# The last block of a routed expert layer: 32 tokens with weights stationary, in place of a half block of 128

## The chip, the cores and the metric

The kernel runs on one core of one Trainium2 chip. The metric is the device time of one execution in microseconds (us). TensorE (PE) multiplies matrices, VectorE (DVE) and ScalarE (ACT) work on elements, GpSimd (POOL) computes and issues indirect DMAs, SyncE (SP) issues the other DMAs. A matmul has a stationary operand, which a weight load (PEld, LDWEIGHTS) brings into the array, and a moving operand, whose columns stream through it.

## The reference

Attention with queries pooled in pairs of neighbouring dimensions, and behind it a mixture of eight experts of which each token takes one. The change is in the experts:

```python
def _moe_ref(x, modality_id, w_gate, modality_bias, w1, w2):
    logits = x @ w_gate + modality_bias[modality_id]
    e_idx = np.argmax(logits, axis=1)
    ...
    gate_w = probs[np.arange(N), e_idx]
    for e in range(E):
        mask = e_idx == e
        h = np.maximum(x[mask] @ w1[e], 0.0)
        out[mask] = gate_w[mask, None] * (h @ w2[e])
```

There are 4608 tokens of 512 floats, eight experts, and 1024 hidden values in each.

## The kernel before, in words

The first two thirds are the attention. From some 740 us on the kernel works on **blocks** of tokens that have one expert. The router on VectorE counts the tokens of each expert. An expert with n tokens gets full blocks of 256, and where a rest remains, either another full block or, for a rest of at most 128, a **half block** of 128 places. The program has a fixed list, `order`: full blocks 0 to 17 and then one half block, `NBF`, which is number 18 in this text. Whatever routing asks for beyond that list goes by a general path behind it, inside `tc.If(more > 0)`; `more` is column 2 of the tile `tot` (L425 to L430). Lists in DRAM name the tokens of each block; places beyond a block's tokens have an index out of range, and the scatter writes nothing for them.

Every product is made in three fp16 matmuls: activations and weights are each split into a high and a low part (`xh`/`xl`, `hi`/`lo`, `hh`/`hl`), and high·high, high·low and low·high are summed in PSUM. Weights arrive as f32 by DMA (`load_w`, from SP) in eight pieces to a block, four for each layer; `split_w` makes their two parts, `hi` on ScalarE (L1268) and `lo` on VectorE (L1269). Second-layer parts rotate through five buffers (`W2B`).

For a full block, `gemm1` makes a quarter of the hidden values with the weights stationary and 256 tokens moving (24 matmuls a quarter, L1285 to L1287); ScalarE writes `hh` by a relu (L1290), VectorE the rest `hl` (L1291). `gemm2` makes the second layer with the hidden values stationary and 512 output columns of the weights moving (L1331 to L1333): a call takes a quarter of the hidden values, and for each of two pieces of it both token halves in turn. `scaled` multiplies one half by the gate on ScalarE (L1339), and `scatter` writes its 128 rows to `out` by an indirect DMA that GpSimd issues (L1342).

`run_blocks` writes the order out by hand: eight steps `s` to a block, four of each layer. Beside them it issues the splits of weights that are needed a block later, DMAs, the gathers of tokens of the block after next (`load_x` at step 3, L1173, on GpSimd), and at step 5 (`T_ST`) the second scatter of the block before. Behind step 7 come both evictions of the block and its first scatter. Inside these blocks no engine is free to reorder; each runs its instructions as written. After block 17, `run_blocks` issues that block's second scatter, a DRAIN on GpSimd (`nc.gpsimd.drain(fusable=False)`, L1410), and the split of the last weight piece.

The half block is then made by `block(NBF)`. Its first layer is `half_gemm1` (L1293 to L1319) with tokens stationary and 256 columns of the weights moving: 48 matmuls, a relu into f32 (L1316), and eight f32 transposes on TensorE (L1304) with their split into `hh` and `hl` (L1306, L1307). Its second layer is `gemm2` for one half: 24 matmuls with 512 columns. One eviction and one scatter follow, and the program ends when that has landed.

Of the kernel before, what the change touches and what calls it, by code (L numbers as in the profile page):

```python
# [9 lines left out]
F32 = mybir.dt.float32  # L10
F32R = mybir.dt.float32r
F16 = mybir.dt.float16
BF16 = mybir.dt.bfloat16
I32 = mybir.dt.int32
# [84 lines left out]
NTT = T // P  # L99
TB = 256  # L100
HB = TB // 2
NBF = (T + E * (HB - 1)) // TB
NBST = 18
WR = 5
# [52 lines left out]
def drain(g):  # L157
    for _ in g:
        pass


class Router:
# [244 lines left out]
    def other_blocks(self):  # L407
        nc, sm = self.nc, self.sm
        rest = sm.tile([P, E], F32, name="rest")
        nc.vector.scalar_tensor_tensor(rest, self.na, -float(TB), self.base, op0=ALU.mult, op1=ALU.add)  # L410
        nc.vector.tensor_single_scalar(rest, rest, float(HB - 1), op=ALU.add)
        counts = sm.tile([P, 2, E], F32, name="nbh")
        nb, nh = counts[:, 0], counts[:, 1]
        self.up_to(rest, nb)
        yield
        nc.vector.scalar_tensor_tensor(nh, nb, -float(TB), rest, op0=ALU.mult, op1=ALU.add)
        nc.vector.tensor_single_scalar(nh, nh, float(HB - 1), op=ALU.is_gt)
        cum = self.running(counts, "cumB")
        cumB, cumH = cum[:, 0], cum[:, 1]
        yield  # L420
        self.ownB = self.owners(cumB, NBF - NA, "B")
        yield
        self.ownH = self.owners(cumH, E, "H")
        self.tot = self.con.tile([P, 3], I32, name="tot")
        nc.vector.tensor_single_scalar(self.tot[:, 0:1], cumB[:, E:E + 1], float(NA), op=ALU.add)  # L425
        nc.vector.tensor_copy(self.tot[:, 1:2], cumH[:, E:E + 1])
        most = sm.tile([P, 2], F32, name="most")
        nc.vector.tensor_scalar(most[:, 0:1], cumB[:, E:E + 1], float(NA), float(NBST), op0=ALU.add, op1=ALU.max)
        nc.vector.tensor_scalar(most[:, 1:2], cumH[:, E:E + 1], 1.0, -float(NBST + 1), op0=ALU.max, op1=ALU.add)
        nc.vector.tensor_tensor(self.tot[:, 2:3], most[:, 0:1], most[:, 1:2], op=ALU.add)  # L430

        yield
        done = sm.tile([P, E], F32, name="done")
        nc.vector.tensor_tensor(done, nb, self.na, op=ALU.add)
        full = sm.tile([P, E], F32, name="fulls")
        nc.vector.tensor_tensor(full, cumB[:, 0:E], self.na, op=ALU.subtract)
        half = sm.tile([P, E], F32, name="halfs")
        nc.vector.tensor_single_scalar(half, cumH[:, 0:E], float(2 * (NBF - NA)), op=ALU.add)
        nc.vector.tensor_single_scalar(half, half, 0.5, op=ALU.mult)
        nc.vector.tensor_tensor(half, half, done, op=ALU.subtract)  # L440
        nc.vector.tensor_tensor(half, half, full, op=ALU.subtract)
        self.done, self.full, self.half = done, full, half
# [756 lines left out]
def experts(tc, ctx, rt, ident, pre, w1, w2, out, side, first):  # L1199
# [93 lines left out]
    def half_gemm1(j):  # L1293
# [24 lines left out]
                turn_h(q - 1)  # L1318
        turn_h(3)  # L1319

    def gemm2(j, q, halves=(0, 1)):
        b = B[j]
        if q == 0 and halves[0] == 0:
            b["po"] = [ps_o.tile([P, DM], F32, name="po") for h in parts(j)]
        hi, lo = b["w", 4 + q]
        for f in range(2):
            c = 2 * q + f
            for h in halves:
                po = b["po"][h]
                hs = slice(h * P, (h + 1) * P)  # L1330
                nc.tensor.matmul(po, b["hh"][:, c, hs], hi[:, f], start=c == 0, stop=False)  # L1331
                nc.tensor.matmul(po, b["hh"][:, c, hs], lo[:, f], start=False, stop=False)
                nc.tensor.matmul(po, b["hl"][:, c, hs], hi[:, f], start=False, stop=c == 7)  # L1333
            beside()
# [3 lines left out]
        o = b["o", h] = xp.tile([P, DM], F32, name=f"o{h}")  # L1338
        nc.scalar.activation(o, b["po"][h], AF.Copy, scale=b["gate"][:, h:h + 1])  # L1339

    def scatter(j, h):
        nc.gpsimd.indirect_dma_start(out=out[:, :], out_offset=bass.IndirectOffsetOnAxis(ap=index(rt, j, h)[1], axis=0),  # L1342
                                     in_=B[j]["o", h][:, :], in_offset=None, bounds_check=T - 1, oob_is_err=False)

    def store(j, halves=(0, 1)):
        for h in halves:
# [13 lines left out]
    def run_blocks():  # L1360

        todo = iter(pieces[NF:])

        def fetch(n=1):
            for _ in range(n):
                p = next(todo, None)
                if p:
                    load_w(*p)

        fetch(WR)  # L1370
        load_x(1)
        for q in range(NF, 4):
            split_w(0, q)
        turn = {1: turn_x(1)}
        fetch(4)
        late = order.index(NA)
        ahead, own = {}, {}
        for m in range(1, len(order)):
            own[m] = T_OWN[m == late] if m in (1, late) else ()
            ahead[m] = () if m in (1, late) else T_AHEAD  # L1380
        for i, j in enumerate(order[:-1]):
            for s in range(8):
                k = 8 * i + 7 + s
                if i == 0 and s < 4:
                    split_w(0, 4 + s)
                    fetch()
                (gemm1 if s < 4 else gemm2)(j, s % 4)
                for _ in range(own[i + 1].count(s)):
                    next(turn[i + 1], None)
                if k > 7:  # L1390
                    split_w(*pieces[k])
                    fetch()
                if i and s == T_ST:
                    scatter(order[i - 1], 1)
                if i + 2 < len(order) and i + 2 != late:
                    if s == GX:
                        load_x(order[i + 2])
                        turn[i + 2] = turn_x(order[i + 2])
                    for _ in range(ahead[i + 2].count(s)):
                        next(turn[i + 2])  # L1400
            drain(turn[i + 1])
            scaled(j, 0)
            scaled(j, 1)
            scatter(j, 0)
            if i + 2 == late:
                drain(side)
                load_x(order[i + 2])
                turn[i + 2] = turn_x(order[i + 2])
        scatter(order[-2], 1)
        nc.gpsimd.drain(fusable=False)  # L1410
        split_w(*pieces[-1])

    def block(j):
        if j >= NBF:
# [8 lines left out]

    with tc.manual_schedule(engines=MAN0):
        run_blocks()
        block(NBF)
    more = nc.values_load(rt.tot[0:1, 2:3], min_val=0, max_val=NBF - NBST + E - 1)  # L1427
    with tc.If(more > 0):
        for col, n, first_, js in ((0, NBF, NBST, range(NBST, NBF)), (1, E, 1, range(NBF + 1, NBF + E))):
            tot = nc.values_load(rt.tot[0:1, col:col + 1], min_val=0, max_val=n)  # L1430
            with ExitStack() as nest:
                for i, j in enumerate(js):
                    nest.enter_context(tc.If(tot > first_ + i))
                    start(j)
                    block(j)
# [111 lines left out]
```

## Time and profile before

| | us |
|---|---|
| median of three runs | 1140.86 (1140.09 to 1142.14) |
| the profiled execution | 1140.92 |
| its span, first to last instruction | 1139.2 |
| TensorE busy | 1110.6 (97%) |
| VectorE, ScalarE, GpSimd busy | 978.9, 915.8, 419.4 |
| mean granted TensorE clock | 0.999 |

The profile is one execution taken by the hardware profiler. In its rows a group reads: line, engine, operation, output<-inputs, shapes, count. Timeline rows begin with start and duration in us; in brackets at the end stand how long the engine had been idle before and what ended that. "POOLq" and the like are an engine's queue of instructions that do not count as work, a DRAIN among them. "issue" is time in which the profile shows no wait.

### The profile page before, as it was taken

To read this page: it belongs to the slowest core of one execution; us is meant where nothing else is said; L and a number is where in the kernel's file an instruction comes from. 1 tells how busy PE (TensorE), PEld (TensorE's weight loads), DVE (VectorE), ACT (ScalarE), POOL (GpSimd) and SP (SyncE) were. 2 spreads that over 40 slices of the span, in tenths; PEclk is the share of its full clock that TensorE was granted. 3 is DMA by queue.
4 is the path that set the end of the run, shared out by engine and by line. 5 is a ranking of instruction groups with operands and counts; after the bars stand their busy time and mean duration, and the time that the engine had idled before them with its cause. 6 is when DMAs were issued, how large, how long until landed. Compare 5 with 4: busy or idle time off the path is not lost. (4 is left out here: it accounts for less than half of the span.)

```text
span 1139.2 us, 36649 instructions
## 1 busy us (share of the span) xinstructions
PE 1110.6 (97%) x15001; PEld 817.0 (72%) x15001; DVE 978.9 (86%) x1962; ACT 915.8 (80%) x1463; POOL 419.4 (37%) x408
## 2 busy tenths in 40 slices
PE   7999999999999999999999989999999999999997
PEld 3777777777777777777777767767677676676674
DVE  7999999999999999999999999888977766667563
ACT  5999999999999999999999988865656656556553
POOL 7854444444444444345344441133222122121211
PEclk9999999999999999999999999999999999999999
DMA  7767867858768659578678563599899999999981
GB/s 230 200 178 170 191 167 167 193 154 193 176 163 207 161 163 201 159 169 186 175 171 181 143 143 76 184 289 274 277 272 255 304 288 280 283 277 272 281 250 65
DMA packets 175568, 232.65 MB, mean 204 GB/s; under 512 B 92351, under 2 KB 126799, under 8 KB 175392
## 3 DMA queue, kind: packets, MB, share of 16 engines
q1 hardware_dynamic: 169254, 210.45, 70.6%
q0 software_dynamic: 6128, 19.78, 6.9%
q8 instruction: 119, 1.95, 0.7%
q14 instruction: 57, 0.47, 0.1%
q10 hardware_dynamic: 10, 0.00, 0.0%
HBM read 146.11 MB, written 19.18 MB: 145 GB/s over the span
## 5 line engine op out<-in xcount | busy, mean ns | idle before, releaser
L881 ACT ACTIVATE Pe<-psc 128x432 int32<-128x432 f32 x768 | 377.9, 527 | 42.0 <-PE psc L880 33.1
L813 DVE TENSOR_REDUCE mp<-pm 128x1 f32<-128x512 f32 x566 | 372.8, 684 | 14.1 <-PE pm L812 6.7
L938 PE MATMUL xp<-VH,Pe 128*128 128x65 f16 x2880 | 372.6, 193 | 0.0
L940 PE MATMUL xp<-VS,Pl 128*128 128x65 f16 x2880 | 371.9, 193 | 0.4 <-DVE Pl L864 0.4
L939 PE MATMUL xp<-vl,Pe 128*128 128x64 f16 x2880 | 370.6, 192 | 0.0
L939 PEld LDWEIGHTS <-Pe 128*128 128x128 f16 x2880 | 267.6, 98 | 87.6
L879 PE MATMUL psc<-B 128*128 128x432 f16 (+2 forms) x1152 | 304.0, 286 | 1.9 <-ACT Pe L881 1.8
L880 PE MATMUL psc<-B 65*128 65x432 f16 (+2 forms) x1152 | 304.7, 287 | 0.0
L938 PEld LDWEIGHTS <-Pe 128*128 128x128 f16 x2880 | 271.9, 98 | 45.2 <-issue 7.0
L940 PEld LDWEIGHTS <-Pl 128*128 128x128 f16 x2880 | 266.5, 97 | 0.6 <-DVE Pl L864 0.5
L862 ACT ACTIVATE Pl<-Pe 128x1152 f16<-128x1152 uint16 (+1 forms) x190 | 219.2, 1154 | 6.0
L812 PE MATMUL pm<-hi,QB 128*128 128x512 f16 x566 | 213.8, 379 | 8.4 <-DVE mp L813 8.1
L674 POOL TENSOR_TENSOR lo<-rawk,hi 128x576 f16<-128x576 f32 (+1 forms) x68 | 87.9, 1296 | 198.0 <-ACT hi L658 186.4
L761 POOL TENSOR_SCALAR VH<-rawv,sc 128x512 f16<-128x512 f32 (+1 forms) x60 | 103.4, 1734 | 153.1 <-PE xp L940 73.8
L1287 PE MATMUL ph<-xpart,w1l 128*128 128x256 f16 x544 | 148.3, 273 | 0.0
L1285 PE MATMUL ph<-xpart,w1h 128*128 128x256 f16 x544 | 148.3, 273 | 0.0
L1286 PE MATMUL ph<-xpart,w1h 128*128 128x256 f16 x544 | 148.3, 273 | 0.0
L880 PEld LDWEIGHTS <-B 65*128 65x128 f16 x1152 | 112.9, 98 | 25.5 <-issue 2.8
L879 PEld LDWEIGHTS <-B 128*128 128x128 f16 x1152 | 112.5, 98 | 9.2 <-issue 3.8
L1291 DVE SCALAR_TENSOR_TENSOR hl<-ph,hh 128x512 f16<-128x512 f32 x72 | 49.7, 691 | 76.2 <-ACT hh L1290 75.9
L1290 ACT ACTIVATE hh<-ph 128x512 f16<-128x512 f32 x72 | 43.0, 598 | 87.3 <-PE ph L1287 87.3
L1333 PE MATMUL po<-w2h,hl 128*128 128x512 f16 x296 | 112.2, 379 | 0.0
(263 smaller groups left out, 1924.8 us busy)
## 6 DMA issues: line engine op xcount, KB each, us to landing
w2r<-in_w_dram SPq DMA_DIRECT2D x76, 512.0 KB
w1r<-in_w_dram SPq DMA_DIRECT2D x72, 512.0 KB
rawv<-in_att_dram SPq DMA_DIRECT2D x32, 576.0 KB
B<-hi SPq DMA_DIRECT2D x128, 144.0 KB
rawq<-in_att_dram SPq DMA_DIRECT2D x31, 576.0 KB
rawk<-in_att_dram SPq DMA_DIRECT2D x31, 576.0 KB
B<-qh SPq DMA_DIRECT2D x128, 72.0 KB
B<-lo SPq DMA_DIRECT2D x64, 144.0 KB
```

The lines of the kernel that those rows point to most:

```text
L812: nc.tensor.matmul(pm, QB[p % 2][:, u], s["hi"][:, t * 512:(t + 1) * 512], start=True, stop=True)
L813: nc.vector.tensor_reduce(mp[:, u, t:t + 1], pm, op=ALU.max, axis=AX.X)
L862: nc.scalar.activation(low, rest, AF.Copy, scale=LOW)
L879: nc.tensor.matmul(o, b1[:, ks], b1[:, qs], start=True, stop=False, skip_group_check=True)
L880: nc.tensor.matmul(o, b2[:, ks], b2[:, qs], start=False, stop=True, skip_group_check=True)
L881: nc.scalar.activation(Pe[:, D + x0:D + x1], pt, AF.Exp, scale=1.0 / 16)
L938: nc.tensor.matmul(out, Ph[:, qs], vh[:, c, j, 0:D + 1], start=c == 0 and g == 0, stop=False, skip_group_check=True)
L939: nc.tensor.matmul(out[:, 0:D], Ph[:, qs], vl[:, c, j], start=False, stop=False, skip_group_check=True)
L940: nc.tensor.matmul(out, Pl[:, qs], vs[:, c, j, 0:D + 1], start=False, stop=c == NKC - 1, skip_group_check=True)
L1285: nc.tensor.matmul(o, hi[:, c, fs], xh[:, :, c], start=c == 0, stop=False)
L1286: nc.tensor.matmul(o, hi[:, c, fs], xl[:, :, c], start=False, stop=False)
L1287: nc.tensor.matmul(o, lo[:, c, fs], xh[:, :, c], start=False, stop=c == 3)
```

## The change

Five edits:

1. In the half block's place stands `few(NBF)`, a block of `MB` = 32 tokens. Its first layer keeps the weights stationary and moves 32 tokens (96 matmuls, each with a weight load); relu and split read PSUM at once, so that no transposes stand between the layers. The second layer also keeps the weights stationary: 128 output columns at a time, with two such groups side by side in one PSUM tile of 128x64 (`po`), twice (96 matmuls). What comes out lies transposed, so ScalarE copies it to f32 (`os`), TensorE transposes it (two a tile), and ScalarE scales it by the gate. The scatter takes 32 rows.
2. Block 17 (`order[-2]`) makes its second layer by token halves: all of half 0 in steps 4 and 5, all of half 1 in steps 6 and 7. Half 0 is evicted and scattered at step 5, half 1 behind step 7; the split of the last weight piece stands ahead of the latter.
3. A DRAIN on GpSimd stands behind the second scatter of each block in the loop, 17 of them. The one that stood ahead of the half block stays, now behind block 17's second scatter.
4. The router computes `over`, by how much the largest rest of a half block exceeds 32, and adds it to `more`.
5. Behind `If(more > 0)`, a rest larger than 32 is made anew as a half block of 128 by the general path.

```diff
+MB = 32
...
-        self.tot = self.con.tile([P, 3], I32, name="tot")
+        self.tot = self.con.tile([P, 4], I32, name="tot")
...
+        part = sm.tile([P, E], F32, name="partial")
+        nc.vector.scalar_tensor_tensor(part, nb, -float(TB), rest, op0=ALU.mult, op1=ALU.add)
+        nc.vector.scalar_tensor_tensor(part, part, 1.0 - HB - MB, nh, op0=ALU.add, op1=ALU.mult)
+        over = sm.tile([P, 1], F32, name="over")
+        nc.vector.tensor_reduce(over, part, op=ALU.max, axis=AX.X)
+        nc.vector.tensor_single_scalar(over, over, 0.0, op=ALU.max)
+        nc.vector.tensor_copy(self.tot[:, 3:4], over)
+        yield
...
-        nc.vector.tensor_tensor(self.tot[:, 2:3], most[:, 0:1], most[:, 1:2], op=ALU.add)
-
+        nc.vector.tensor_tensor(most[:, 0:1], most[:, 0:1], most[:, 1:2], op=ALU.add)
+        nc.vector.tensor_tensor(self.tot[:, 2:3], most[:, 0:1], over, op=ALU.add)
...
+    def few(j):
+        b = B[j]
+        ts = slice(0, MB)
+        hh, hl = (xp.tile([P, 8, TB], F16, name=x)[:, :, ts] for x in ("hh", "hl"))
+        xh, xl = b["xh"][:, 0, :, ts], b["xl"][:, 0, :, ts]
+        for q in range(4):
+            hi, lo = b["w", q]
+            ph = ps_h.tile([P, 2, TB], F32, name="ph")[:, :, ts]
+            for f in range(2):
+                fs = slice(f * P, (f + 1) * P)
+                for c in range(4):
+                    nc.tensor.matmul(ph[:, f], hi[:, c, fs], xh[:, c], start=c == 0, stop=False)
+                    nc.tensor.matmul(ph[:, f], hi[:, c, fs], xl[:, c], start=False, stop=False)
+                    nc.tensor.matmul(ph[:, f], lo[:, c, fs], xh[:, c], start=False, stop=c == 3)
+            o = slice(2 * q, 2 * q + 2)
+            nc.scalar.activation(hh[:, o], ph, AF.Relu)
+            nc.vector.scalar_tensor_tensor(hl[:, o], ph, 0.0, hh[:, o], op0=ALU.max, op1=ALU.subtract)
+        turned = []
+
+        def turn_o(i, os):
+            px = ps_h.tile([P, 2, TB], F32, name="ph").rearrange("p f n -> p (f n)")[ts, 0:2 * P].rearrange("p (f n) -> p f n", f=2)
+            for f in range(2):
+                nc.tensor.transpose(px[:, f], os[:, f], ident)
+            turned.append(px)
+
+        made = []
+        for i in range(2):
+            po = ps_o.tile([P, DM], F32, name="po")[:, 0:2 * MB].rearrange("p (f n) -> p f n", f=2)
+            for c in range(8):
+                hi, lo = (w[:, c % 2] for w in b["w", 4 + c // 2])
+                for f in range(2):
+                    fs = slice((2 * i + f) * P, (2 * i + f + 1) * P)
+                    nc.tensor.matmul(po[:, f], hi[:, fs], hh[:, c], start=c == 0 and f == 0, stop=False, skip_group_check=True)
+                    nc.tensor.matmul(po[:, f], hi[:, fs], hl[:, c], start=False, stop=False, skip_group_check=True)
+                    nc.tensor.matmul(po[:, f], lo[:, fs], hh[:, c], start=False, stop=c == 7, skip_group_check=True)
+                if made and c == 2:
+                    turn_o(*made.pop())
+            os = xq.tile([P, 2, MB], F32, name="os", bufs=2)
+            nc.scalar.copy(os, po)
+            made.append((i, os))
+        turn_o(*made.pop())
+        o = b["o", 0] = xp.tile([P, DM], F32, name="o0")
+        for i, px in enumerate(turned):
+            nc.scalar.activation(o[ts, 2 * i * P:2 * (i + 1) * P], px.rearrange("p f n -> p (f n)"), AF.Copy, scale=b["gate"][ts, 0:1])
+        scatter(j, 0, MB)
...
-                (gemm1 if s < 4 else gemm2)(j, s % 4)
+                if s < 4:
+                    gemm1(j, s)
+                elif j == order[-2]:
+                    for q in range(s % 2 * 2, s % 2 * 2 + 2):
+                        gemm2(j, q, (s // 2 - 2,))
+                else:
+                    gemm2(j, s % 4)
...
                 if i and s == T_ST:
                     scatter(order[i - 1], 1)
+                    nc.gpsimd.drain(fusable=False)
+                    if j == order[-2]:
+                        store(j, (0,))
...
+            if j == order[-2]:
+                split_w(*pieces[-1])
+                store(j, (1,))
+                break
...
-        scatter(order[-2], 1)
         nc.gpsimd.drain(fusable=False)
-        split_w(*pieces[-1])
...
-        block(NBF)
-    more = nc.values_load(rt.tot[0:1, 2:3], min_val=0, max_val=NBF - NBST + E - 1)
+        few(NBF)
+    more = nc.values_load(rt.tot[0:1, 2:3], min_val=0, max_val=NBF - NBST + E - 1 + HB - MB)
     with tc.If(more > 0):
+        wide = nc.values_load(rt.tot[0:1, 3:4], min_val=0, max_val=HB - MB)
+        with tc.If(wide > 0):
+            B[NBF] = {}
+            start(NBF)
+            block(NBF)
```

What ScalarE has to do from block 17's last first-layer weights of the next block to its last eviction. `w2h` are the high parts of the second-layer weights, `o` evictions of token halves; line 1268 of before is 1277 of the change, and 1339 is 1395. Before:

```order
L1268 ACTIVATE w1h_23169<-w1r 128x1024
L1268 ACTIVATE w2h<-w2r 128x1024 x3
L1339 ACTIVATE o_23224<-po,gate 128x512
L1339 ACTIVATE o_23226<-po,gate 128x512
L1268 ACTIVATE w2h<-w2r 128x1024
L1316 ACTIVATE hs<-ph 128x256 x2
L1306 CAST hh<-px 128x2x128
L1316 ACTIVATE hs<-ph 128x256
L1306 CAST hh<-px 128x2x128
L1316 ACTIVATE hs<-ph 128x256
L1306 CAST hh<-px 128x2x128 x2
L1339 ACTIVATE o_23343<-po,gate 128x512
```

and now:

```order
L1277 ACTIVATE w1h_23193<-w1r 128x1024
L1277 ACTIVATE w2h<-w2r 128x1024
L1395 ACTIVATE o_23217<-po,gate 128x512
L1277 ACTIVATE w2h<-w2r 128x1024 x3
L1395 ACTIVATE o_23258<-po,gate 128x512
L1346 ACTIVATE hh<-ph 128x2x32 x4
L1369 COPY os<-po 128x64 x2
L1374 ACTIVATE o_23482<-ph,gate 32x256 x2
```

The first half's eviction of block 17 moved ahead of three weight splits, and the second half's stands behind all of them; then come four relus, two copies and two small evictions in place of nine operations.

On TensorE, the hand-over from block 17's last matmuls to the small block's first. `po` is block 17's output in PSUM, `xpart` the tokens of the last block, `w1h0` and `w1l0` its first weight piece; for a matmul the moving operand stands ahead of the stationary one. Before:

```order
L1332 LDWEIGHTS hh_23029
L1332 MATMUL po_23156<-w2l_23059,hh_23029 128x512
L1333 LDWEIGHTS hl_23030
L1333 MATMUL po_23156<-w2h_23058,hl_23030 128x512
L1313 LDWEIGHTS xpart_22995
L1313 MATMUL ph_23242<-w1h0_23089,xpart_22995 128x256
L1314 LDWEIGHTS xpart_22996
L1314 MATMUL ph_23242<-w1h0_23089,xpart_22996 128x256
```

and now:

```order
L1388 LDWEIGHTS hh_23053
L1388 MATMUL po_23180<-w2l_23083,hh_23053 128x512
L1389 LDWEIGHTS hl_23054
L1389 MATMUL po_23180<-w2h_23082,hl_23054 128x512
L1342 LDWEIGHTS w1h0_23113
L1342 MATMUL ph_23266<-xpart_23019,w1h0_23113 128x32
L1343 LDWEIGHTS w1h0_23113
L1343 MATMUL ph_23266<-xpart_23020,w1h0_23113 128x32
L1344 LDWEIGHTS w1l0_23114
L1344 MATMUL ph_23266<-xpart_23019,w1l0_23114 128x32
```

Tokens and weights changed sides: the weight load now brings in weights, and 32 tokens move where 256 weight columns did. The last matmuls of block 17 are the same.

On GpSimd the rows keep their order; a DRAIN is added behind each block's second scatter, which is ahead of the next block's first scatter and of the gathers after it.

More of the change, by code (lines that the diff above doesn't have):

```diff
@@ L1339, in scaled, with scatter @@
         nc.scalar.activation(o, b["po"][h], AF.Copy, scale=b["gate"][:, h:h + 1])
-    def scatter(j, h):
-        nc.gpsimd.indirect_dma_start(out=out[:, :], out_offset=bass.IndirectOffsetOnAxis(ap=index(rt, j, h)[1], axis=0),
-                                     in_=B[j]["o", h][:, :], in_offset=None, bounds_check=T - 1, oob_is_err=False)
+    def scatter(j, h, n=P):
+        nc.gpsimd.indirect_dma_start(out=out[:, :], out_offset=bass.IndirectOffsetOnAxis(ap=index(rt, j, h)[1][0:n], axis=0),
+                                     in_=B[j]["o", h][0:n, :], in_offset=None, bounds_check=T - 1, oob_is_err=False)
     def store(j, halves=(0, 1)):
```

## The prediction

> **What bounds the kernel now.** I read the page's first part, then the last 40 us of the trace in windows, then the chain of waits, then single rows of the tail.
>
> ```profile
> span 1139.2 us, 36649 instructions
> PE 1110.6 (97%) x15001; PEld 817.0 (72%) x15001; DVE 978.9 (86%) x1962; ACT 915.8 (80%) x1463; POOL 419.4 (37%) x408
> ```
>
> TensorE is busy for 97% of the span, so time is to be won where it has fewer or cheaper matmuls, or at the end, where it has none. The profiled execution took 1140.92 us: its span of 1139.2 and 1.72 us beside it. The sum below is made against that execution; it lies 0.06 us above the median of the three runs (1140.86), so nothing has to be corrected between them.
>
> ```profile
> 1100.00:1110.00 10.00, 10.00 (x94) 8.98 (x92) 5.00 (x6) 5.41 (x8) 2.01 (x2) 1.00 0.81 218
> 1110.00:1120.00 10.00, 10.00 (x50) 4.71 (x49) 7.30 (x7) 5.43 (x6) 0.00 (x0) 1.00 0.45 149
> 1120.00:1130.00 10.00, 9.02 (x71) 6.75 (x69) 2.92 (x5) 4.87 (x11) 1.94 (x2) 1.00 0.14 52
> 1130.00:1140.00 10.00, 3.38 (x16) 1.35 (x14) 0.00 (x0) 0.69 (x1) 0.97 (x1) 0.80 0.03 9
> ```
>
> A row gives a stretch, its length, the busy time and instructions of TensorE, weight loads, VectorE, ScalarE and GpSimd, then the granted clock, the DMA share and GB/s. TensorE is full through the last full block (17, to 1120.7), DMA nearly idle from 1120 on, and the half block (18) alone behind that. In the timeline:
>
> ```profile
> 1120.51 0.38 PE L1333 MATMUL po<-w2h,hl 128*128 128x512 f16 x1
> 1120.73 0.27 PE L1313 MATMUL ph<-w1h,xpart 128*128 128x256 f16 x1
> ...
> 1127.77 0.44 PE L1304 MATMUL px<-ident,hs 128*128 128x128 f32 x2 [0.98 <-DVE hl L1307]
> 1128.04 0.38 PE L1331 MATMUL po<-w2h,hh 128*128 128x512 f16 x1
> 1128.24 0.37 ACT L1306 CAST hh<-px 128x256 f16<-128x256 f32 x1 [0.99 <-PE px L1304]
> ...
> 1133.00 0.38 PE L1333 MATMUL po<-w2h,hl 128*128 128x512 f16 x1
> 1133.47 0.69 ACT L1339 ACTIVATE o<-po,gate 128x512 f32<-128x512 f32 x1 [4.86 <-PE po L1333]
> 1134.43 0.97 POOL L1342 DMA_INDIRECT out_dram<-o,siB  x1 [8.73 <-ACT o L1339]
> ```
>
> So the half block costs 13.70 us from its first matmul (1120.73) to its scatter (1134.43): its first layer, a stall at the last transposes, 24 matmuls at 0.2155 us (23 steps from 1128.04 to 1133.00), one eviction. Behind the scatter's start are 4.77 us to the span's end. The chain of waits, though, names no matmul there:
>
> ```profile
> 1124.50 1.19 POOLq L1410
> 1125.70 6.24 issue
> ...
> 1134.47 0.93 POOL out_dram L1342
> ```
>
> It runs through GpSimd's DRAIN (L1410). That row is this:
>
> ```profile
> L1410 POOLq DRAIN  x1: 7403/7403/7403, 1124.5 to 1124.5; - x1
> L1542 POOLq DRAIN  x3: 46/107/153, 1137.5 to 1138.7; - x3
> ```
>
> Rows that end in "-; - x1" give the form; ahead of it stand the durations (least, median, most, in ns) and the first and last start. L1542 is the program's end. The DRAIN at L1410 ends at 1131.90 (1124.50 + 7.40); the half block's output is ready only at 1134.16 (1133.47 + 0.69): so far the DRAIN is covered with 2.26 us to spare. A small block that is quicker by more than that uncovers it. This is the second thing on which the forecast turns.
>
> **The matmuls of the small block.** Removed: 48 matmuls with 256 moving columns, eight f32 transposes and 24 matmuls with 512. Added: 96 and 96 matmuls with 32 moving columns, each with a weight load of its own, and four transposes. Short moving operands with a load each stand elsewhere in the trace:
>
> ```profile
> 758.01 0.60 PE L266 MATMUL pmr<-wgs,xt 128*128 128x24 bf16 x18
> 758.46 0.38 PE L1331 MATMUL po<-w2h,hh 128*128 128x512 f16 x1
> ...
> 401.21 0.19 PE L938 MATMUL xp<-VH,Pe 128*128 128x65 f16 x1
> 401.24 0.19 PE L939 MATMUL xp<-vl,Pe 128*128 128x64 f16 x1
> L1286 PEld LDWEIGHTS <-w1h x576: 97/98/101, 740.2 to 1110.0; 128*128 128x128 f16 x192
> ```
>
> Eighteen pairs with 24 columns take 758.01 to 758.46, which is 0.45/18 = 25 ns a pair (the last of them ends at 758.61, so one lasts some 0.17); two pairs with 65 and 64 columns start 30 ns apart. One weight load is recorded at 98 ns, so loads must overlap each other. That gives the pair from 25 ns below to 98 ns above, if for 192 in a row the loads did not overlap. I take 26, beside the nearest row (24 columns). Layer 1: 96 × 0.026 = 2.5 us, 1120.73 to 1123.23. Layer 2 has twice 48 × 0.026 = 1.25 us and, in between, two transposes, for which I take the 0.27 us between 1127.77 and 1128.04: 1123.23 to 1126.0.
>
> The Trainium skill's page "TensorE: Matmul & The Clock Gate", section "Back-to-back issue gap", speaks against the change: it gives a stream of weight load and matmul pairs about 81 ns each at 128 columns and 131 at 512, and says that a single matmul's gap under-counts such a stream for want of the loads. By 81 ns, 192 pairs would take an estimated 15.6 us. The trace does not bear it out: 25 ns a pair in the row above, and at 512 columns 216 ns as above, not 131.
>
> Does layer 2 wait for layer 1's evictions? Durations by shape:
>
> ```profile
> L1290 ACT ACTIVATE hh<-ph 128x512 f16<-128x512 f32 x72 | 43.0, 598 | 87.3 <-PE ph L1287 87.3
> L1306 ACT CAST hh<-px 128x256 f16<-128x256 f32 x4 | 1.5, 368 | 1.0 <-PE px L1304 1.0
> L1291 DVE SCALAR_TENSOR_TENSOR hl<-ph,hh 128x512 f16<-128x512 f32 x72 | 49.7, 691 | 76.2 <-ACT hh L1290 75.9
> L1307 DVE TENSOR_TENSOR hl<-px,hh 128x256 f16<-128x256 f32 x4 | 1.7, 425 | 3.6 <-ACT hh L1306 3.6
> ```
>
> On the line through both sizes, 128x64 takes about 0.25 us on ScalarE (0.368 − 192 × 0.9 ns = 0.20 below; I allow 0.25) and 0.23 on VectorE. The last group's matmul starts at 1123.2 and lasts some 0.17; then 0.25, 0.23 and two hand-overs below 0.1 us: hl is there at about 1123.95. Layer 2 reads it first behind 36 of its first 48 matmuls, at 1123.23 + 36 × 0.026 = 1124.17. No stall; without that cover it would cost some tenths.
>
> From the last matmul (done at 1126.17): ScalarE copies 128x64, to 1126.42, then come two transposes and ScalarE's second scaling. Before, it read a transposed pair 0.47 us behind the pair's start (the pair at 1127.77 was read at 1128.24). With 0.05 for the hand-over, 1126.47 + 0.47 + 0.37 (the row of 128x256) = 1127.31. The scatter before started 0.27 behind the eviction's end (1134.16 to 1134.43), so here at **1127.6**, which is 6.8 us earlier than 1134.43, if GpSimd is free.
>
> **Block 17 by token halves.** The matmuls are the same 48. Their order is what changes: the first half's output is done at 1110.37 + 24 × 0.2155 = 1115.54, and its eviction and scatter go ahead by some 4.5 us. What is late instead are the weights of block 18:
>
> ```profile
> 1110.37 0.38 PE L1331 MATMUL po<-w2h,hh 128*128 128x512 f16 x1
> ...
> 1116.52 1.06 ACT L1268 ACTIVATE w2h<-w2r 128x1024 f16<-128x1024 f32 x1 [1.57 <-DMA w2r<-in_w_dram]
> 1117.61 1.23 DVE L1269 SCALAR_TENSOR_TENSOR w2l<-w2r,w2h 128x1024 f16<-128x1024 f32 x1 [0.83 <-ACT w2h L1268]
> 1121.24 0.97 POOL L1342 DMA_INDIRECT out_dram<-o,siB  x1 [14.89 <-ACT o L1339]
> 1124.73 0.97 POOL L1342 DMA_INDIRECT out_dram<-o,siB  x1 [2.51 <-ACT hh L1306]
> ...
> DMA to landing us min/median/max: 2.6/2.6/2.7
> ```
>
> There are five buffers for second-layer weights, so three of block 18's four pieces wait until block 17's are read for the second time, at 1115.54 + 6, 12 and 18 matmuls: 1116.85, 1118.1 and 1119.4. The last split is then 1119.5 to 1120.5 on ScalarE and to 1121.8 on VectorE, where layer 2 wants it after 1124. Behind that split stands the second half's eviction, which waits for the last matmul anyway (1120.51): 0.69 us, to 1121.6. Its scatter starts at about 1121.9; before, the pair's second had to wait for the first and started at 1124.73. That brings the last DRAIN forward by 2.8 us. The layer-1 evictions wait for this one until 1121.6, while the first group of 24 is done at 1121.5: no loss, and of three PSUM buffers the fourth group needs the first at 1122.6.
>
> **The DRAINs.** Seventeen are added, one behind each block's second scatter. Of their length the trace has only the two rows above: 7.4 us with 36 scatters issued since the start, at most 0.15 us at the end with one. I bound each by 0.05 and 7.4 us; a DRAIN does no work that something else is spared, so none of them gains.
>
> ```profile
> 863.02 1.49 POOL L1342 DMA_INDIRECT out_dram<-o,siA  x1 [0.30 <-issue]
> 871.59 1.27 POOL L1342 DMA_INDIRECT out_dram<-o,siA  x1 [7.09 <-ACT o L1339]
> ```
>
> Behind a loop DRAIN on GpSimd stand the next block's first scatter and, behind that, two gathers. The tightest gap is this one, 8.57 us from scatter to scatter, in which GpSimd waited 7.09 us for ScalarE. A DRAIN of 7.4 behind 863.3 ends at 870.7 and fits. So I price the 17 at nothing; without that cover, each would push gathers back by what it overhangs. Of the last DRAIN, I take the short length: with two scatters issued since the DRAIN before it instead of 36, it is nearest to the row with one. It would then end soon after the second half has landed (1121.9 + 2.6 = 1124.5), before 1127.6.
>
> **Routing.** Seven VectorE instructions more, of 128x8 or 128x1:
>
> ```profile
> 792.29 0.15 DVE L428 TENSOR_SCALAR most<-cumB 128x1 f32<-128x1 f32 x1
> ```
>
> 7 × 0.16 = 1.1 us once, in the middle of the blocks; block weights are split long ahead there, so I price it between 0 and 1.1, at 0. The general path runs only if the part block holds over 32 tokens. The last scatter moves 80 packets and 0.01 MB, while two whole ones move 160 and 0.52; rows of 512 floats have 2 KB, so it is some 5 tokens, and the path is not taken.
>
> ```profile
> q0 software_dynamic: 80, 0.01, 0.6%
> ...
> q0 software_dynamic: 160, 0.52, 13.6%
> ```
>
> **The sum.** Scatter 1134.43 − 6.8 = 1127.6, and 4.77 behind it: span 1132.4; with 1.72, **1134.1 us**.
>
> **Rivals.**
> A: the DRAIN keeps its length, and becomes the bound. It ran to 1131.90, 7.17 us from its scatter's start at 1124.73. From 1121.9 that is 1129.07; from a release to a scatter's start the tail has 0.27 us (above) and 0.89 (landing at 1121.24 + 2.6 = 1123.84, next scatter 1124.73). By the longer one the scatter is at 1129.96, a gain of 4.5, **1136.4**. For: one row of 7.4 us is all that shows a DRAIN behind a scatter in flight. Against: that scatter's data was down 4.6 us before the DRAIN's end, so it didn't wait for this alone, and the last ones are short.
> B: TensorE's supply. The trace shows 18 short pairs in a row, never 192.
>
> ```profile
> 735.20:740.20 5.00, 5.00 (x127) 4.50 (x127) 4.12 (x11) 3.18 (x6) 1.60 (x2) 1.00 0.97 312
> ```
>
> The densest 5 us I found have 127 pairs, 39 ns each. If that is a limit on how fast instructions reach TensorE, 192 × (39 − 26) ns = 2.5 us come on top: **1136.6**. Against: matmuls with 512 columns stand among the 127, which set that pace by themselves.
> C, slower: weight loads do not overlap in a long run. 192 × 98 ns = 18.8 us instead of 5.0: scatter at 1127.6 + 13.8 = 1141.4, **1147.9**. It decides from the pace at which the gain of 6.8 is gone, 26 + 6800/192 = 61 ns. (By the 81 ns of the Trainium skill's section named above, the same sum would be an estimated 1144.7.) Against C: the 25 and 30 ns above, so it keeps little.
> D: the block doesn't fit 32 tokens, or loop DRAINs far above 7.4 us starve the gathers: over 1141. The rows speak against both.
>
> **How the numbers follow.** Forecast 0.60, A 0.25, B 0.08, a pace between B's and C's 0.03, C 0.03, D 0.01. The forecast's own range is 1132.8 (small pieces gone as well) to 1135 (30 ns a pair, a short stall). To leave out no more than 2 in 10 I must take in A: 1132.8 to 1137.3, which has B's time too. A measurement tells about 0.2% here, 2.3 us; forecast, A and B lie 4.3 to 6.8 us below 1140.9: faster 0.93; the pace between gives within 0.03; C and D slower 0.04.
>
> **What would show it.** The small block's first 96 matmuls span 2.5 us and its last starts near 1126; its scatter starts near 1127.6; the last DRAIN is well below 5 us and the one behind each block too. A is right if it is 7 us and the chain runs through it; B if rows of this block start 50 ns apart with nothing waited for; C if 98. If loop gathers start later than before relative to their block, D. I am wrong altogether if the time is above 1138.6.

## The result, and the profile after

| | before | the change |
|---|---|---|
| median, us | 1140.6 (1140.09 to 1142.14, 4 runs) | 1134.76 (1133.65 to 1135.75, 4 runs) |
| ratio | | 0.9945, 95% interval 0.9932 to 0.9957 |
| the profiled execution, us | 1140.92 | 1135.75 |
| its span, us | 1139.2 | 1134.0 |

The forecast was 1134.1, its range 1132.8 to 1137.3: direction, size and mechanism came as forecast. The sum, however, holds an error of 0.8 us at its end, and one of its covers was thinner than it said; that it lies within 0.7 us of the median is in part luck, as is worked out behind the experiments. No run here has a rest above 32 tokens, so the price of the general path is not measured. The page of the change, first part:

```profile
span 1134.0 us, 36903 instructions
PE 1105.3 (97%) x15117; PEld 814.7 (72%) x15117; DVE 979.1 (86%) x1968; ACT 914.1 (81%) x1462; POOL 417.2 (37%) x408
```

The windows of the end, columns as before:

```profile
1110.00:1120.00 10.00, 10.00 (x55) 5.18 (x53) 6.55 (x7) 6.33 (x8) 0.97 (x1) 1.00 0.61 199
1120.00:1130.00 10.00, 7.35 (x205) 5.96 (x203) 3.65 (x7) 4.21 (x11) 1.89 (x2) 1.00 0.10 34
1130.00:1140.00 10.00, 0.00 (x0) 0.00 (x0) 0.00 (x0) 0.00 (x0) 0.00 (x0) 0.71 0.02 3
```

TensorE has 205 matmuls where 71 stood, in less time, and nothing behind 1130. The timeline of the small block:

```profile
1121.55 0.38 PE L1389 MATMUL po<-w2h,hl 128*128 128x512 f16 x1
1121.76 0.18 PE L1342 MATMUL ph<-xpart,w1h 128*128 128x32 f16 x1
...
1124.14 0.18 PE L1344 MATMUL ph<-xpart,w1l 128*128 128x32 f16 x1
1124.16 0.18 PE L1363 MATMUL po<-hh,w2h 128*128 128x32 f16 x1
...
1126.78 0.18 PE L1365 MATMUL po<-hh,w2l 128*128 128x32 f16 x1
1126.99 0.21 ACT L1369 COPY os<-po 128x64 f32<-128x64 f32 x1 [1.23 <-PE po L1365]
1127.10 1.05 ACT L1374 ACTIVATE o<-ph,gate 32x256 f32<-32x256 f32 x2
1127.26 0.39 PE L1353 MATMUL ph<-ident,os 128*32 128x128 f32 x2 [0.30 <-ACT os L1369]
1128.43 0.92 POOL L1398 DMA_INDIRECT out_dram<-o,siB  x1 [4.53 <-ACT o L1374]
```

The first 96 matmuls take 2.40 us (1121.76 to 1124.16), 25.0 ns each, and no row among the 192 shows a wait. From the first of them to the last scatter are 6.67 us, where the half block took 13.70. GpSimd's DRAINs, in the loop (L1457) and ahead of the last scatter (L1478):

```profile
L1457 POOLq DRAIN  x17: 3866/5610/9413, 774.2 to 1105.8; - x17
...
L1478 POOLq DRAIN  x1: 3230/3230/3230, 1122.7 to 1122.7; - x1
```

The last one ends at 1125.92, and GpSimd then waits until 1128.2 for the output, as this piece of the chain of waits shows:

```profile
1122.69 1.21 POOLq L1478
1123.90 2.06 issue
...
1126.05 2.15 issue
```

**Where the 5.2 us of span come from.** The small block gives 13.70 − 6.67 = 7.03. Two terms go the other way. The small block began at 1121.76, the half block at 1120.73: 1.03 us. It arises ahead of all that the change adds to the blocks, since block 0's first scatter is as late already (765.46 and 766.48, ahead of the first DRAIN and of the router's new instructions). Whether the change has a part in it stays open: that scatter stands at 764.34 to 765.61 in the four profiles with the half block and at 765.28 to 768.08 in the ten with the small one. And behind the last scatter's start are 5.57 us instead of 4.77: 0.80. 7.03 − 1.03 − 0.80 = 5.20, which is 1139.2 − 1134.0.

From block 0's first scatter to the small block's first matmul it is 355.27 us before and 355.28 in the change, and 355.18 to 355.28 in every other version below but few_old_order (354.31). There only that scatter was later: from block 1's first matmul (764.93 before, 765.96 in the change) to the last block's it is 355.8 us in all fourteen profiles. All that was added between, 17 DRAINs, the router's instructions, the other order in block 17, costs nothing that can be seen. The profiles differ ahead of it, by up to 3.7 us (764.34 to 768.08), so below the tails are compared from the small block's first matmul on.

### The profile page after: what moved, and what is told of

Read it like the earlier page. It is cut to its first block, busy times and chain, and to the rows that moved or that the text cites. A ratio compares the mean times of both kernels' runs of the same rounds, so it can differ in the third digit from the quotient of the medians.

```text
span 1134.0 us, 36903 instructions
## 1 busy us (share of the span) xinstructions
PE 1105.3 (97%) x15117; PEld 814.7 (72%) x15117; DVE 979.1 (86%) x1968; ACT 914.1 (81%) x1462; POOL 417.2 (37%) x408
## 5 line engine op out<-in xcount | busy, mean ns | idle before, releaser
L1389 PE MATMUL po<-w2h,hl 128*128 128x512 f16 x288 | 109.1, 379 | 0.0
```

## The experiments

Every ratio is to before, with its 95% interval. "Tail" is the time from the last block's first matmul to its scatter, and to the end of the span: 13.70 and 18.47 before, 6.67 and 12.24 in the change.

**Are the loop's DRAINs needed?** Two versions of the change: without the 17, and without any.

```diff
                 if i and s == T_ST:
                     scatter(order[i - 1], 1)
-                    nc.gpsimd.drain(fusable=False)
```

> The change without the 17 DRAINs in the loop; the one ahead of the last scatter stays. Theory G (a DRAIN waits for the landing of the scatter ahead of it and then takes time for every GpSimd DMA issued since the last DRAIN): with some 75 DMAs since the start it ends about 4.5 us behind the landing, as before the change (7.4 us after its start), so some 7.4 to 7.7 us long; the last scatter then starts some 2.2 to 2.6 us later than in the change's profile relative to TensorE's first small matmul (8.9 to 9.3 us behind it instead of 6.67), and the median is about 1137, 3.5 us below before. Rival L (a DRAIN waits for the landing alone): 3.2 us long, last scatter 6.7 us behind the first small matmul, median as the change, 5.8 us below before.

Measured: 1138.43 us, ratio 0.9966 (0.9954 to 0.9979). Tail 9.66 and 15.54. The DRAIN's row and the last scatter's:

```profile
L1477 POOLq DRAIN  x1: 7822/7822/7822, 1124.3 to 1124.3; - x1
```
```profile
1133.02 0.91 POOL L1398 DMA_INDIRECT out_dram<-o,siB  x1 [7.52 <-issue]
```

Theory G holds in its mechanism, at 7.8 us and a tail 0.4 longer than expected, though the DRAIN ended 3.1 us behind the landing (1129.0) and not 4.5. The output is ready at 1129.76, and the scatter starts 0.9 us behind the DRAIN's end at 1132.1: the mechanism of the prediction's rival A, with 9.66 us of tail where its sum has 9.23.

```diff
-        nc.gpsimd.drain(fusable=False)
```

(Both places.)

> The change without any DRAIN. Theory (the change's last DRAIN is covered, and the loop ones too): same time as the change, 5.8 us below before, last scatter 6.7 us behind TensorE's first small matmul. Rival (the loop DRAINs cost time by holding gathers or scatters back, or the last one still binds): faster than the change by more than 1 us.

Measured: 1141.51 us, ratio 1.0001 (0.9990 to 1.0012). Neither theory: the whole gain is gone. The scatter starts 6.67 us behind the first small matmul, as in the change, but the program's end has GpSimd drained as well:

```profile
L1612 POOLq DRAIN  x3: 40/107/6286, 1132.6 to 1139.4; - x3
```

The first of those three DRAINs takes 6.29 us here, with nothing in flight any more; in the change the longest is 0.13. So the DRAIN is work that is due once, and a DRAIN earlier in the program only settles where it is done. Before the change it lay beside the half block's matmuls.

**The DRAINs alone**, with the half block as it was:

```diff
                     scatter(order[i - 1], 1)
+                    nc.gpsimd.drain(fusable=False)
```

> Before with the 17 DRAINs in the loop alone; half block and order of block 17 stay. Theory: the DRAIN ahead of the last scatter shrinks from 7.4 to some 3.0 to 3.8 us; as it was covered by 2.3 us and the loop's are covered too, the time is that of before (within 0.7 us), last scatter 13.7 us behind the first matmul of the half block. Rival (the loop's DRAINs hold gathers or scatters back): slower by 1 us or more.

Measured: 1141.03 us, ratio 1.0003 (0.9992 to 1.0014), tail 13.70 to the scatter. As expected:

```profile
L1411 POOLq DRAIN  x1: 3068/3068/3068, 1124.7 to 1124.7; - x1
```

**What sets a DRAIN's length?** One DRAIN in the loop, in block 9, 13 or 5:

```diff
                     scatter(order[i - 1], 1)
-                    nc.gpsimd.drain(fusable=False)
+                    if i == 9:
+                        nc.gpsimd.drain(fusable=False)
```

> The change with one DRAIN in the loop, in block 9, in place of 17. Theory G2 (a DRAIN takes some 85 ns for every GpSimd DMA since the last one, counted from the end of the last scatter's issue, and not less than to that scatter's landing; 85 ns is 6.29 us over the 76 DMAs that the program's end drained in the version without DRAINs): some 31 DMAs stand between, 2.6 us, so the last DRAIN is 3.7 to 4.2 us long, still covered, and the time is that of the change. Rival G1 (the time per DMA comes on top of the landing): 3.2 + 31 x 0.06 = 5.1 us long, last scatter some 0.3 us later. Rival H (its length comes from the first use of DRAIN, or it is fixed from the second on): 3.2 us, as in the change. The DRAIN in block 9 itself, with some 42 DMAs behind it, is 4.8 us or longer under G2 and G1.

> The change with one DRAIN in the loop, in block 13. The last DRAIN so far, from the end of the issue of the scatter ahead: 2.0 us with 4 DMAs since the one before (ends with the landing), 5.0 with some 32 (one in block 9), 6.2 to 6.6 with some 75 (none). Theory P (time for every DMA since the last DRAIN): with some 18, 2.5 to 4.2. Rival H (short only if a DRAIN stands in the block before): 5 us or more.

> The change with one DRAIN in the loop, in block 5. Theory P (time for every DMA since the last DRAIN): with some 48, 5.2 to 6.0 us from the end of the issue of the scatter ahead to the DRAIN's end, between the 5.0 of one in block 9 and the 6.2 to 6.6 of none. Rival S (a fixed number of DMAs is kept, and beyond some 30 it grows no more): 4.9 to 5.1 us.

Measured: 1134.66 us, ratio 0.9941 (0.9921 to 0.9961); 13 and 5, one run each, 1134.87 and 1135.24 us. The last DRAIN with one in block 9, in 13 and in 5:

```profile
L1479 POOLq DRAIN  x1: 6158/6158/6158, 1122.0 to 1122.0; - x1
```
```profile
L1479 POOLq DRAIN  x1: 3999/3999/3999, 1121.9 to 1121.9; - x1
```
```profile
L1479 POOLq DRAIN  x1: 6526/6526/6526, 1121.9 to 1121.9; - x1
```

None of the sizes given for block 9 was met; those of theory P for 13 and 5 were (2.8 and 5.3 us from the end of the issue), without saying how the length grows. So this was worked out anew from the DRAINs with many DMAs, each against the landing of the scatter ahead of it (start plus the profile's time to landing) and the number of GpSimd DMAs since the last DRAIN (2 ahead of the change's last one, the two scatters of block 17, and not the 4 of the expectation for block 13):

| DRAIN | DMAs | landing | DRAIN's end | behind it, us | each, ns |
|---|---|---|---|---|---|
| the change, last | 2 | 1125.8 | 1125.9 | 0.1 | |
| block 13 only, last | 15 | 1125.25 | 1125.9 | 0.65 | 43 |
| block 5 only, in the loop | 28 | 868.7 | 869.9 | 1.2 | 43 |
| block 9 only, last | 31 | 1126.8 | 1128.15 | 1.35 | 44 |
| block 9 only, in the loop | 44 | 944.1 | 946.0 | 1.85 | 42 |
| block 5 only, last | 47 | 1126.45 | 1128.4 | 1.95 | 42 |
| block 13 only, in the loop | 60 | 1028.8 | 1031.35 | 2.55 | 43 |
| none in the loop, last | 75 | 1129.0 | 1132.1 | 3.1 | 41 |
| before | 75 | 1127.4 | 1131.9 | 4.5 | 60 |

In seven rows the DRAIN ends 41 to 44 ns behind the landing for every DMA since the last one. Before the change it was 60 ns, and two further versions below that keep the half block and 75 DMAs (half_halves_only, half_rows32) have the same 4.4 to 4.5 us. In these three the scatter had landed 1.8 us behind the end of its issue, in the seven rows 2.1 to 4.4 us behind it; and with nothing in flight it was 6.29 us for 76, 83 ns each. One account fits all of them: some 41.5 ns for every DMA as soon as the last issue has ended, and as much again behind the landing, or behind the first pass where that ends later. Before, that gives 1125.70 + 2 × 75 × 0.0415 = 1131.9; with one in block 9, 1126.8 + 31 × 0.0415 = 1128.1; with none, 2 × 76 × 0.0415 = 6.3 us. It was fitted to these rows, and no run was made to test it. Rivals H and S are out, since it grows from 15 to 75. In time, one DRAIN in block 9 does as well as the 17, although it holds the last scatter back by 1.3 us; why that cost nothing is told below.

**Block 17 by halves**, alone and taken out of the change:

```diff
-                (gemm1 if s < 4 else gemm2)(j, s % 4)
+                if s < 4:
+                    gemm1(j, s)
+                elif j == order[-2]:
+                    for q in range(s % 2 * 2, s % 2 * 2 + 2):
+                        gemm2(j, q, (s // 2 - 2,))
...
```

> Before with block 17's second layer by token halves alone; the half block of 128 and its one DRAIN stay. Theory: the second scatter of block 17 starts some 2 to 2.8 us earlier and with it the DRAIN, still 7.2 to 7.4 us long, both covered by the half block's matmuls; same time as before (within 0.5 us), last scatter 13.7 us behind the first matmul of the half block. Rival (the late weight splits stall the half block): slower by up to 1.5 us.

Measured: 1141.71 us, ratio 1.0004 (0.9996 to 1.0013), tail 13.70 to the scatter, DRAIN 7.41 us from 1121.3. As expected: alone it is worth nothing.

```diff
...
-                    if j == order[-2]:
-                        store(j, (0,))
...
+        scatter(order[-2], 1)
         nc.gpsimd.drain(fusable=False)
+        split_w(*pieces[-1])
```

> The change with block 17's second layer, evictions, scatters and last split in the order of before. Theory: the second of block 17's scatters waits for the landing of the first and starts about 4.0 us behind TensorE's first small matmul (before: 1124.73 against 1120.73), its landing comes 2.7 to 2.9 us later, the DRAIN ends with it, at 6.9 to 7.1, and the last scatter starts about 7.3 to 7.6 us behind the first small matmul instead of 6.67: 0.6 to 0.9 us slower than the change. Rival (the halves are worth nothing): 6.7 us, same time as the change.

Measured: 1136.23 us, ratio 0.9954 (0.9940 to 0.9968), whose interval overlaps with the change's; the traces separate them. Tail 8.31 and 13.51, so 1.27 us worse than the change at the end, more than expected, and two things stand behind it. The first is the theory's. The DRAIN and the scatter behind it:

```profile
L1470 POOLq DRAIN  x1: 3615/3615/3615, 1125.0 to 1125.0; - x1
```
```profile
1129.50 0.91 POOL L1398 DMA_INDIRECT out_dram<-o,siB  x1 [3.32 <-ACT o L1374]
```

The DRAIN ends at 1128.60, 7.4 us behind the first small matmul and not 6.9 to 7.1. The row names ScalarE, whose output is ready at 1129.05. But from that output to the scatter's start it is 0.28 us in the change and 0.45 here, whereas from a DRAIN's end it is 0.90 to 0.91 us in the three versions where the DRAIN was plainly last (none in the loop, block 9 only, block 5 only), and 0.90 here. So the DRAIN was last. ScalarE's output, however, was only some 0.2 us ahead of it: alone it would have put the scatter at an estimated 1129.05 + 0.28 = 1129.33. This is the second thing, which the theory did not have. TensorE had waited, in the small block's first layer, for VectorE:

```profile
1124.47 0.18 PE L1342 MATMUL ph<-xpart,w1h 128*128 128x32 f16 x1 [1.33 <-DVE hl L1347]
```
```profile
1123.06 1.23 DVE L1278 SCALAR_TENSOR_TENSOR w2l<-w2r,w2h 128x1024 f16<-128x1024 f32 x1 [4.53 <-ACT w2h L1277]
1124.20 0.48 DVE L1347 SCALAR_TENSOR_TENSOR hl<-ph,hh 128x64 f16<-128x64 f32 x3
```

The old order evicts both halves ahead of the last weight split on ScalarE, so VectorE gets to its part at 1123.06 only, and the small block's first split `hl` stands behind it. The fourth group of matmuls needs that PSUM buffer. In the change the same queue was met in time by a hair:

```profile
1119.16 3.81 DVE L1278 SCALAR_TENSOR_TENSOR w2l<-w2r,w2h 128x1024 f16<-128x1024 f32 x3 [2.49 <-ACT w2h L1277]
1122.90 0.22 DVE L1347 SCALAR_TENSOR_TENSOR hl<-ph,hh 128x64 f16<-128x64 f32 x1
```

`hl` starts at 1122.90, when VectorE is free, and ends at 1123.12; the fourth group starts at 1123.57, 0.45 us later.

**Is it the 32 rows that land later?** The last scatter's landing took 2.6 us before and 3.6 in the change. Tried both ways: 32 rows with the half block, 128 with the small one.

```diff
...
-            store(j, (h,))
+            scaled(j, h)
+            scatter(j, h, 32 if j == NBF else P)
```

> Before with 32 rows in the half block's scatter instead of 128 and nothing else. Profiles so far have 2.4 to 2.6 us from the start of the last scatter to its landing with 128 rows and 3.1 to 3.8 with 32. Theory (the number of rows sets this): 3.1 to 3.8 us, and the time is 0.5 to 1 us above before. Rival (something else of the small block, such as the shorter time since the scatter ahead): 2.4 to 2.7, time as before.

```diff
+        o = b["o", 0] = xp.tile([P, DM], F32, name="o0")
+        nc.vector.memset(o, 0.0)
...
-        scatter(j, 0, MB)
+        scatter(j, 0)
```

> The change with 128 rows in the last scatter, the other 96 of them zeros (VectorE clears the tile while it is idle) whose indices are out of range. Theory (the number of rows sets the landing): 2.4 to 2.7 us from the last scatter's start to its landing instead of 3.1 to 3.8, time 0.5 to 1 us below the change. Rival: 3.1 to 3.8 us as in the change, same time.

Measured: 1141.07 us, ratio 1.0004 (0.9990 to 1.0019), landing 2.4; and 1135.55 us, ratio 0.9944 (0.9928 to 0.9961), landing 3.4. The rows are not it. What does go with a late landing are instruction packets on the DMA engines. In the change they pass in the half microsecond in which the scatter's first do:

```profile
q8 instruction: 1, 0.02, 17.0%
q0 software_dynamic: 16, 0.01, 13.0%
```

That is 1129.5 to 1130.0, and single packets of the scatter come up to a microsecond behind the rest. Before, that large packet started at 1134.7 and was through at 1135.6, and the scatter's came from 1135.9 on. Over all 14 profiles, that packet starts 1.0 to 1.7 us behind the start of the last scatter in the seven with a landing of 3.1 us or more, and at most 0.5 behind it in the seven with 2.1 to 2.7.

**What sets the end?** The engines load `more` and branch past the general path. This is the branch's line in the change:

```profile
L1495 PEldq EVENT_SEMAPHORE  x2: 51/51/51, 1132.4 to 1132.6; - x2
...
L1495 PEldq COMPARE_BRANCH  x1: 3802/3802/3802, 1128.6 to 1128.6; - x1
...
L1495 POOLq INC_SWDGE_SEM  x1: 203/203/203, 1132.2 to 1132.2; - x1
```

TensorE's sequencer needs 3.8 us for it and is done, with two semaphores, at 1132.6; GpSimd, which waits for the landing, at 1132.4. With one DRAIN in block 9 the last scatter had started 1.3 us later than in the change (7.99 behind the first small matmul) and the span ended at 12.27, as in the change: a delay of the scatter that cost nothing. That fits a branch that ends last, but also what the trace shows of the landing, which took 2.3 us there and not 3.6, so that it came 10.3 us behind the first small matmul instead of 10.2. To tell, the load was moved ahead:

```diff
+    early = []
...
                     for q in range(s % 2 * 2, s % 2 * 2 + 2):
                         gemm2(j, q, (s // 2 - 2,))
+                    if s == 5:
+                        early.append(nc.values_load(rt.tot[0:1, 2:3], min_val=0, max_val=NBF - NBST + E - 1 + HB - MB))
...
-    more = nc.values_load(rt.tot[0:1, 2:3], min_val=0, max_val=NBF - NBST + E - 1 + HB - MB)
+    more = early[0]
```

> The change with the load of `more` on every engine moved from behind the small block into block 17 (behind step 5); the branch on it stays at the end. Theory F (what ends last in the change is not the scatter but TensorE's branch: it loads `tot` from 1127.3 to 1128.5, branches at 1128.6 for 3.8 us, and the program's end follows at 1134.0, 12.24 us behind the first small matmul): TensorE branches at some 5.2 to 5.4 us behind its first small matmul instead of 6.85 and is done at 9.1; the scatter's landing (6.67 + 2.4 to 3.6, then 0.3) becomes the last, the span ends 11.0 to 12.0 us behind the first small matmul, and the time is 0.2 to 1.2 us below the change. If TensorE's queue doesn't hide the load, a gap of up to 1.2 us stands among block 17's matmuls. Rival (the scatter's landing ends last, whatever TensorE's branch does): 12.2 us, time of the change.

> The change itself once more, beside the others of this call. First small matmul to the last scatter 6.6 to 6.8 us; TensorE's branch 3.4 to 3.9 us long, span's end 12.0 to 12.4 us behind the first small matmul; median 1134 to 1136.

Measured: 1134.13 us, ratio 0.9938 (0.9922 to 0.9954), against 1135.77 us, ratio 0.9949 (0.9932 to 0.9966), for the change beside it. The intervals overlap. The traces separate them: the change's tail is 6.66 and 12.24 again, that of the early load 6.67 and 11.13. Its branch, and its landing:

```profile
L1498 PEldq COMPARE_BRANCH  x1: 3590/3590/3590, 1127.7 to 1127.7; - x1
...
L1498 POOLq INC_SWDGE_SEM  x1: 199/199/199, 1131.5 to 1131.5; - x1
```

The branch starts 5.5 us behind the first small matmul instead of 6.8, and the landing takes 2.5 us instead of 3.6. No gap stands in block 17, where TensorE does the load 8 us ahead of the small block. Branch and landing came forward together, but what stands behind them tells which was last. SyncE's waits at the end, in the change and with the early load:

```profile
L1614 SPq EVENT_SEMAPHORE  x14: 17/28/28, 1132.4 to 1134.0; - x14
```
```profile
L1617 SPq EVENT_SEMAPHORE  x14: 17/28/28, 1131.7 to 1133.3; - x14
```

Both begin 0.4 us behind the landing (1132.0 and 1131.3) and take 1.6 us, though TensorE was done 0.2 us behind their beginning in the change and 0.2 ahead of it with the early load. In all nine profiles of the small block with a DRAIN ahead of the last scatter, the span ends 2.0 us behind the landing; behind the end of TensorE's branch it ends anywhere from 1.6 to 4.9 us. So the landing was last in each, and theory F had the wrong one. Its rival did not foresee that the landing itself would take 2.5 us instead of 3.6, which is the 1.1 us gained. The branch was close behind in the change, so that a quicker landing alone might have gained less; that wasn't tried. This version has the shortest tail of all.

## Why the prediction was right, step by step

- **Pace of the matmuls: right.** 26 ns were taken, 25.0 measured over 96 in a row. Rivals B (39) and C (98) are out; against B the text counted on matmuls with 512 columns among its 127, where the trace has 144 to 432. Out, too, is the rule of the Trainium skill's page "TensorE: Matmul & The Clock Gate", section "Back-to-back issue gap", as applied here: 192 pairs of weight load and matmul came at 25 ns each, not 81. The loads, recorded at 98 ns, overlap four deep or so.
- **From first matmul to scatter: right to 0.2.** 6.67 us, 6.87 forecast.
- **No stall from layer 1's evictions: right, but the cover was misnamed.** The text counted ScalarE's eviction and three PSUM buffers; what comes last is VectorE's weight split in front of `hl`. 0.45 us were left. few_old_order shows the price without: a wait of 1.33 us.
- **The last DRAIN: right, and the step on which all hangs.** The forecast took the short length, because few DMAs would have been issued since the DRAIN before. It ended 0.1 us behind the landing; without the loop's DRAINs it took 7.8 us and bound the scatter, which was rival A's mechanism. Wrong was the sentence beside it that a DRAIN spares nothing else any work: the loop's take over what the last one, or else the program's end, would have to do, which the two rows of before could not show.
- **The loop's DRAINs cost nothing: right**, 355.28 us against 355.27. They are 3.9 to 9.4 us long, more than the 7.4 taken as a bound; the one in the tightest gap took 8.0, which the 8.57 us still held.
- **The halves: right, with one effect missed.** Second scatter 1.16 us behind the small block's first matmul, 1.17 forecast. Alone they are worth nothing; with the small block 1.27 us of the tail, through the DRAIN, as forecast, and through the order of weight splits, which the prediction saw as a risk of the halves and not as a gain. In few_old_order the two came out within 0.2 us of each other.
- **"4.77 behind it": wrong by 0.8.** The end was taken as a constant behind the scatter's start. It follows the scatter's landing, by 2.2 us before and 2.0 in the change, and the landing took 3.6 us instead of 2.6. The prediction had no term for that; why it took longer is not shown.
- **The sum: near the median with some luck.** Against the profiled execution, 1135.75 us, the forecast of 1134.1 is 1.65 short: 1.03 for the later start of the blocks and 0.80 at the end, less the 0.20 of the tail. The four executions of the change spread from 1133.65 to 1135.75, and the profiled one was the slowest.

## What to carry to other kernels

When a block at the end gets quicker, list what had run beside it for nothing: here a DRAIN, weight splits in another engine's queue, and the load and branch behind the last instruction. Each found a new place (a DRAIN in the loop, another order, an early load). Without DRAINs in the loop the ratio was 0.9966 in place of 0.9945, without any DRAIN the gain was nought. And compare tails from a point that no edit touches: 355.8 us from block 1's first matmul to the last block's were the same in all profiles, while what lies ahead of them differed by 3.7.

## What the runs showed of the hardware that was not expected

- A DRAIN on GpSimd took some 43 ns behind the landing of the last DMA for every DMA that GpSimd issued since the DRAIN before (seven rows, 15 to 75 DMAs), 60 where that landing came early, and the program's end does it if nothing did before (6.29 us for 76).
- TensorE's sequencer took 3.43 to 3.92 us for one branch over code that isn't run; ScalarE's row for the same branch shows 0.05 us, but its next instruction came 3.0 us after it before the change (1134.5 to 1137.5) and 3.4 in it (1128.7 to 1132.1). The Trainium skill's page "Runtime: NRT & Kernel Launch", section "Instruction fetch mechanics", says that instructions are fetched ahead in sequence, in blocks of 16 KiB, and that a taken branch out of the window of two such blocks stalls until its target has been fetched. The packets of 0.02 MB at these branches agree; no run here took the skipped code away to show it.
- Instruction packets that pass while a small scatter is under way go with a landing about 1 us later, in seven profiles of fourteen. Where the scatter came later by itself (one DRAIN in block 9 or 5) and the packets had passed, it landed in 2.3 and 2.1 us. Only the early load moved the packets, and it moved the branches too, so the cause is argued and not shown.
